# One of 47 FFN groups back from seven products to eight, its weight differences four slots later, and five filling matmuls instead of thirteen

## The chip, the cores and the metric

The kernel runs on one core of a Trainium2 chip. The metric is the device time of one execution in microseconds (us), of which the median over several runs is taken. One further execution is recorded by the hardware profiler; its rows give the durations used below. The core's engines are named as in the profile: PE (TensorE's matmuls), PEld (its weight loads), DVE (VectorE), ACT (ScalarE), POOL (GpSimd) and SP (SyncE, here only a queue that issues DMAs).

## The reference

```python
def _attn_ref(x, filt_r, filt_i):            # x: 8 x 3008 x 256
    X = np.fft.rfft(x, axis=1)
    F = (filt_r + 1j * filt_i)[None, :, :]
    return np.fft.irfft(X * F, n=x.shape[1], axis=1).astype(np.float32)

def _moe_ref(x, w_in, w_out):                # w_in 256 x 2048, w_out 2048 x 256
    h = np.maximum(x @ w_in, 0.0)
    return (h * h @ w_out).astype(np.float32)

# out = _moe_ref(_attn_ref(x, filt_r, filt_i).reshape(24064, 256), moe_w_in, moe_w_out)
```

A filter is applied to each of the 8 sequences in the frequency domain, along the 3008 tokens; then all 24064 tokens go through a feed-forward network (FFN) with a squared ReLU between its two matrices.

## The kernel before, in words

The Fourier transforms are done as matmuls with constant tables, in units: `unit_a` and `unit_b` go forward, `unit_b` multiplies on DVE with the filter (tile `prod`, L421) and POOL adds the two halves of a product by DMA, `unit_p` begins the way back and writes it to HBM (`dZ`), and `unit_y` ends it: it takes a tile `zt`, read back from `dZ` by `read_z` on SP's queue, and gives 376 of the 3008 tokens of `yt`, the FFN's input, in half of the 256 features (L497 on PE, L504 on ACT or L506 on DVE).

The FFN goes over 47 groups of 512 tokens, in slots, eight to a group. In slot 8g + k, `ffn_g1(g, k)` computes 256 of the 2048 hidden values of group g with four matmuls of 512 columns ("G1" below, L527, into `psH`), and ACT takes their ReLU into `h2` (L531, named `h` in the profile). In every second slot `ffn_sq` squares four tiles of `h2` on DVE (L538).

The second matrix comes a group later and in one of two forms. Groups in `SEVEN` take a seven-product form (Winograd's variant of Strassen's): token halves and hidden-tile parities make four quadrants, and so do the tile parity and column halves of W_out. `sums(g, k)` builds four sums and differences of quadrants of `h2` on DVE (L613 to L622, 128 x 2048 each), `products(g, k, s)` does 7 x 16 matmuls of 128 columns one slot later than the plain form would (L642), and the outputs `top` and `bot` are put together by four copies on ACT and three adds on DVE (L649 to L663). The differences of W_out (`sT`) that these products need are made once by `make_t`, four DVE subtractions of 128 x 1024 (L594). The other groups, before the change only the last, take the plain form: `ffn_g2` does eight matmuls of 256 columns per slot, 64 in all (L547), half of the hidden tiles in each slot, and `ffn_out` copies the result on ACT (L558) and stores it.

The order on every engine is the order of the program. The loop over the slots (L810) calls, in this order: `ffn_g1`, the Fourier units planned for the first half of the slot, `make_t` in its four slots, `products` or `ffn_g2`, the units planned for the second half, `ffn_out`, `sums`, `ffn_sq`, and the stores due. The plan (`fft_plan`) gives each unit its half slot by hand-written due times. For the first sequence, `unit_y` for n = 4 to 15 lies in slots 4 to 23, and n = 8 in slot 10; the second sequence's `unit_b` begins in slots 13, 14, 15 and 16.

Before the loop stands a prologue that transforms the first sequence. At its end, `read_z(0, 0)` and `read_z(0, 1)` are issued on SP; POOL waits for the first half of the first of them (`tiny`, L793) and then issues the two halves of the load of W_out (L321), which converts to 16 bits on the way. PE does `unit_a` for the second sequence, then 13 matmuls of zero weights with 512 columns into a bank that nobody reads (`fill`, L800), then `unit_y(0, 0)` to `unit_y(0, 3)`, and the loop begins.

PSUM tiles in the tag `psF` have two buffers, shared by `unit_b`, `unit_p` and `unit_y`; `psO` has two as well, for the outputs of both forms of the second matrix.

Of the kernel before, what the change touches and what calls it, by code (L numbers as in the profile page):

```python
# [110 lines left out]
def kernel(  # L111
# [16 lines left out]
    NG = T // TG  # L128
# [28 lines left out]
    def psF(name):  # L157
        return pps.tile([128, 512], F32, tag="psF", name=name, bufs=2)
# [352 lines left out]
    def ffn_g1(g, s):  # L511
        if s == 0:
            h2s[g] = p_h2.tile([128, NJT, TG], F16, tag="h2", name=f"h2_{g}")
        h2 = h2s[g]
        ps = psH(f"psH_{g}_{s}")
        segs = []
        t = g * TG
        while t < (g + 1) * TG:
            b, r = divmod(t, S)
            n = min((g + 1) * TG - t, S - r)  # L520
            segs.append((t - g * TG, b, r, n))
            t += n
        for i in range(2):
            jt = 2 * s + i
            for o, b, r, n in segs:
                for dt in range(2):
                    nc.tensor.matmul(ps[:, i, o:o + n],  # L527
                                     sWin[:, dt, jt * 128:(jt + 1) * 128],
                                     yts[b][:, dt, r:r + n],
                                     start=(dt == 0), stop=(dt == 1))  # L530
        nc.scalar.activation(out=h2[:, 2 * s:2 * s + 2, :], in_=ps, func=AF.Relu)  # L531

    def ffn_sq(g, s):
        n = 1 if g == NG - 1 else 2
        if (s + 1) % n:
            return
        v = h2s[g][:, 2 * (s + 1 - n):2 * s + 2, :]
        nc.vector.tensor_mul(out=v, in0=v, in1=v)  # L538

    def ffn_g2(g, s):  # L540
        t, half = divmod(s, 2)
        if s % 4 == 0:
            pso[g] = psO(f"psO_{g}_{s}")
        elif g == NG - 1 and half == 0:
            pso[g] = psF(f"psO_{g}_{s}").rearrange("p (a d) -> p a d", d=256)
        for jt in range(8 * half, 8 * half + 8):
            nc.tensor.matmul(pso[g][:, t % 2, :], h2s[g][:, jt, t * 128:(t + 1) * 128],  # L547
                             sWout[:, jt, :], start=(jt == 0), stop=(jt == NJT - 1))

    def ffn_out(g, s):  # L550

        step = 1 if g == NG - 1 else 2
        if (s + 1) % (2 * step):
            return
        n = s // 2 + 1 - step
        ost = p_out.tile([128, 2, 256], F32, tag="ost", name=f"ost_{g}_{s}")
        h0 = n % 2
        nc.scalar.copy(out=ost[:, h0:h0 + step, :], in_=pso[g][:, h0:h0 + step, :])  # L558
        store(g, n, step, ost)

    def store(g, n, step, ost):

        h0 = n % 2
        t0 = g * TG + n * 128
        if step == 2 and t0 // CLS == (t0 + 255) // CLS:
            pieces = [(0, 128, slice(0, 2), t0)]
        else:
            pieces = []
            for h in range(h0, h0 + step):
                a = t0 + 128 * (h - h0)  # L570
                cut = min(-a % CLS, 128) or 128
                pieces += [(p0, p1, h, a + p0) for p0, p1 in ((0, cut), (cut, 128)) if p1 > p0]
        for p0, p1, h, t in pieces:
            b, t = divmod(t, S)
            r, q = divmod(t, CLS)
            v = out[b * S:b * S + S, :].rearrange("(q r) c -> r q c", r=8)[r]
            if p1 - p0 == 128 and h != 0 and h != 1:
                nc.sync.dma_start(out=v[q:q + 256, :].rearrange("(h p) c -> p h c", p=128), in_=ost)
            else:
                nc.sync.dma_start(out=v[q:q + p1 - p0, :], in_=ost[p0:p1, h, :])  # L580
# [4 lines left out]
    def make_t(k):  # L585

        w = sWout.rearrange("p (q e) c -> p q e c", e=2)
        b11, b12 = w[:, :, 0, 0:128], w[:, :, 0, 128:256]
        b21, b22 = w[:, :, 1, 0:128], w[:, :, 1, 128:256]
        if k == 0:  # L590
            sg["t"] = p_t.tile([128, 4, 8, 128], F16, tag="t", name="sT")
        t = sg["t"]
        i0, i1 = ((b12, b11), (b22, t[:, 0]), (b22, b12), (b21, t[:, 1]))[k]
        nc.vector.tensor_sub(out=t[:, k], in0=i0, in1=i1)  # L594
        sg["w"] = {1: b11, 2: b21, 3: b22, 4: t[:, 3], 5: t[:, 0], 6: t[:, 1], 7: t[:, 2]}
# [5 lines left out]
    def sums(g, k):  # L601

        if k not in (0, 1, 2, 4):
            return
        a11, a12, a21, a22 = quads(g)
        if k == 0:
            sg[g] = {1: a11, 2: a12, 4: a22}
        f = sg[g]
        if k in (0, 2):
            f["s"] = p_x32.tile([128, 2, 8, D], F16, tag="x32", name=f"sum_{g}_{k}")  # L610
        t = f["s"][:, 0 if k in (0, 2) else 1]
        if k == 0:
            nc.vector.tensor_add(out=t, in0=a21, in1=a22)  # L613
            f[5] = t
        elif k == 1:
            nc.vector.tensor_sub(out=t, in0=f[5], in1=a11)  # L616
            f[6] = t
        elif k == 2:
            nc.vector.tensor_sub(out=t, in0=a11, in1=a21)  # L619
            f[7] = t  # L620
        else:
            nc.vector.tensor_sub(out=t, in0=a12, in1=f[6])  # L622
            f[3] = t
# [7 lines left out]
    def products(g, k, s):  # L631

        f = sg[g]
        for p, m0, m1 in PARTS[k]:
            if p == 1 and m0 == 0:
                f["x"] = psO(f"psX_{g}").rearrange("p a (t c) -> p a t c", t=2)
            if p == 2 and m0 == 0:
                f["y"] = psO(f"psY_{g}").rearrange("p a (t c) -> p a t c", t=2)
            o = f["x"][:, 0] if p in (1, 6, 7, 4) else f["y"][:, 0 if p == 2 else 1]
            for m in range(m0, m1):  # L640
                q, t = divmod(m, 2)
                nc.tensor.matmul(o[:, t, :], f[p][:, q, 128 * t:128 * t + 128], sg["w"][p][:, q, :],  # L642
                                 start=(m == 0 and p in (1, 2)), stop=(q == 7),
                                 skip_group_check=True)
            if m1 < 16:
                continue
            if p == 1:
                f["top"] = p_out.tile([128, 2, 256], F32, tag="ost", name=f"top_{g}")
                nc.scalar.copy(out=f["top"][:, :, 0:128], in_=o)  # L649
            elif p == 6:  # L650
                nc.scalar.copy(out=f["top"][:, :, 128:256], in_=o)
            elif p == 7:
                f["bot"] = p_out.tile([128, 2, 256], F32, tag="ost", name=f"bot_{g}")
                nc.scalar.copy(out=f["bot"][:, :, 128:256], in_=o)
            elif p == 2:
                for v, i in ((f["top"][:, :, 0:128], 0), (f["bot"][:, :, 128:256], 1)):
                    nc.vector.tensor_add(out=v, in0=f["y"][:, i], in1=v)  # L657
            elif p == 4:
                nc.scalar.copy(out=f["bot"][:, :, 0:128], in_=o)
                stores.append((s + 1, g, 2, f["bot"]))  # L660
            elif p == 3:
                v = f["top"][:, :, 128:256]
                nc.vector.tensor_add(out=v, in0=o, in1=v)  # L663
                stores.append((s + 1, g, 0, f["top"]))
# [64 lines left out]
    def run(plan, s, place):  # L729
        for f, *a in plan.get(2 * s + place, ()):  # L730
            f(*a)
# [64 lines left out]
    for c in range(4):  # L796
        unit_a(1, c)
    ps = psF("fill")
    for _ in range(13):
        nc.tensor.matmul(ps, zero, sSB[:, 0:4, :].rearrange("p a b -> p (a b)"),  # L800
                         start=True, stop=True)
    for n in range(4):
# [1 line left out]
    prologue[0] = False  # L804
    read_z(0, 2)

    SEVEN = range(NG - 1)
    work = fft_plan()

    for s in range((NG + 1) * SLOTS):  # L810
        g, k = divmod(s, SLOTS)
        if g < NG:
            ffn_g1(g, k)
        run(work, s, 0)
        if 8 <= s < 12:
            make_t(s - 8)
        if (s - 1) // SLOTS - 1 in SEVEN:
            products((s - 1) // SLOTS - 1, (s - 1) % SLOTS, s)
        if g > 0 and g - 1 not in SEVEN:
            ffn_g2(g - 1, k)  # L820
        run(work, s, 1)
        if g > 0 and g - 1 not in SEVEN:
            ffn_out(g - 1, k)
        if g - 1 in SEVEN:
            sums(g - 1, k)
        if g < NG:
            ffn_sq(g, k)
        while stores and stores[0][0] <= s:
            _, i, n, ost = stores.pop(0)
            store(i, n, 2, ost)  # L830
# [30 lines left out]
```

## Time and profile before

| | before |
|---|---|
| median of 4 runs | 758.73 us (758.31 to 759.98) |
| the profiled execution's own time | 759.1 us |
| its span, first to last instruction | 757.3 us |
| mean granted TensorE clock | 0.998 |
| busy: PE / DVE / ACT / POOL | 737.8 / 657.1 / 564.8 / 191.6 us |
| fills run from, to | 44.4 to 49.0 us |
| slot 0 begins (first G1 matmul) | 50.45 us |
| products of group 0 begin / of group 1 | 61.63 / 79.23 us |
| last group's plain products | 746.40 to 753.6 us |

Times within the profile count from the span's start. A busy share says how long an engine had an instruction under way; matmuls are pipelined, so that a busy PE need not be at its peak. "Idle before" in a row is the time that the engine waited ahead of it, and behind the arrow stands the instruction or transfer whose end released it. PEclk is the clock that TensorE was granted as a share of its full rate. The DMA share is the mean busy share of the core's 16 DMA engines; where many transfers overlap it can exceed 1.

### The profile page before, as it was taken

The page shows a single profiled execution, that of the slowest core. Times are in us where ns is not written, and L with a number is a line of the kernel's source. Part 1 is how long each engine was busy: PE and PEld are TensorE (multiplying, and loading weights), DVE is VectorE, ACT ScalarE, POOL GpSimd, SP SyncE. Part 2 cuts the span into 40 slices and gives each one's busy share as a digit, 9 for nine tenths or more (in the row PEclk, how much of TensorE's full clock was granted, in tenths as well). Part 3 has the DMA queues.
Part 4 walks back from the last instruction along what each step waited for, and adds up shares of the span by engine and source line. Part 5 has one row for each costly group of instructions (what it writes and reads, how often), then busy time and mean ns, then how long its engine had stood idle before and what let it go on. Part 6 is the DMA issues. An engine that isn't in the chain of part 4 may idle for free.

```text
span 757.3 us, 20205 instructions
## 1 busy us (share of the span) xinstructions
PE 737.8 (97%) x8511; PEld 536.3 (71%) x8511; DVE 657.1 (87%) x731; ACT 564.8 (75%) x808; POOL 191.6 (25%) x265
## 2 busy tenths in 40 slices
PE   7888999999999999999999999999999999999997
PEld 5535766777777777877678777787777777777776
DVE  5959998899899898989979998999988989888783
ACT  4867788778878777787777778777786777777773
POOL 2811750244222321232304224033311222000000
PEclk9999999999999999999999999999999999999999
DMA  9995898566785557746586546764447333321011
GB/s 351 306 192 172 143 184 234 163 118 120 165 221 120 96 128 176 181 103 136 105 219 128 125 100 135 230 130 101 103 113 200 81 77 92 98 86 42 30 57 57
DMA packets 103491, 106.36 MB, mean 140 GB/s; under 512 B 10352, under 2 KB 93552, under 8 KB 102248
## 3 DMA queue, kind: packets, MB, share of 16 engines
q1 hardware_dynamic: 83960, 81.83, 35.6%
q0 software_dynamic: 19296, 23.05, 21.5%
q8 instruction: 67, 1.10, 0.6%
q10 hardware_dynamic: 144, 0.18, 0.1%
q14 instruction: 24, 0.20, 0.1%
HBM read 57.80 MB, written 48.23 MB: 140 GB/s over the span
## 4 chain that ended last, share of the span: by engine, by line
PE 89%; DVE 5%; DMA 2%; ACT 2%; issue 1%; SPq 0%; DVEq 0%
PE psH L527 40%; PE psX L642 20%; PE psY L642 16%; PE psB L412 3%; PE psY L497 2%; PE psP L461 2%; PE psA L347 2%; DVE prod L421 1%; DMA zt<-dZ 1%; DMA xw<-in_x_dram 1%; DVE h L538 1%; PE psO L547 1%; ACT h L531 1%; PE psf L286 1%; PE fill L800 1%
## 5 line engine op out<-in xcount | busy, mean ns | idle before, releaser
L531 ACT ACTIVATE h<-psH 128x1024 f16<-128x1024 f32 x376 | 385.4, 1026 | 160.8 <-PE psH L527 159.8
L527 PE MATMUL psH<-yt,sWin 128*128 128x512 f16 (+7 forms) x1728 | 386.8, 351 | 1.2 <-ACT h L531 0.4
L538 DVE TENSOR_TENSOR h<-h 128x2048 f16<-128x2048 f16 (+1 forms) x192 | 230.1, 1199 | 45.6 <-ACT h L531 45.3
L429 POOL DMA_DIRECT2D prod<-prod x168 | 138.8, 968 | 429.3 <-DVE prod L421 426.9
L527 PEld LDWEIGHTS <-sWin 128*128 128x128 f16 x1728 | 149.1, 98 | 90.5 <-issue 3.0
L642 PEld LDWEIGHTS <-sum 128*128 128x128 f16 x2944 | 181.3, 98 | 26.2 <-issue 6.3
L642 PEld LDWEIGHTS <-h 128*128 128x128 f16 x2208 | 135.6, 98 | 24.5 <-issue 5.4
L421 DVE TENSOR_TENSOR prod<-psB,sF 128x1024 f16<-128x1024 f32 x84 | 102.4, 1220 | 11.9 <-PE psB L412 11.8
L642 PE MATMUL psX<-sT,sum 128*128 128x128 f16 x1472 | 104.7, 219 | 0.0
L642 PE MATMUL psY<-sT,sum 128*128 128x128 f16 x736 | 71.2, 219 | 0.0
L642 PE MATMUL psY<-sWout,sum 128*128 128x128 f16 x736 | 56.0, 219 | 1.4 <-DVE bot L657 1.4
L616 DVE TENSOR_TENSOR sum<-sum,h 128x2048 f16<-128x2048 f16 x46 | 56.2, 1221 | 0.8
L642 PE MATMUL psY<-sWout,h 128*128 128x128 f16 x736 | 56.2, 219 | 0.0
L642 PE MATMUL psX<-sT,h 128*128 128x128 f16 x736 | 56.1, 219 | 0.0
L622 DVE TENSOR_TENSOR sum<-h,sum 128x2048 f16<-128x2048 f16 x46 | 56.1, 1219 | 0.0
L619 DVE TENSOR_TENSOR sum<-h 128x2048 f16<-128x2048 f16 x46 | 56.0, 1218 | 0.0
L195 POOL DMA_DIRECT2D x<-in_x_dram x64 | 55.9, 1046 | 0.5 <-PE psA L347 0.5
L613 DVE TENSOR_TENSOR sum<-h 128x2048 f16<-128x2048 f16 x46 | 55.9, 1216 | 0.0
L463 ACT CAST ze<-psP 128x512 f16<-128x512 f32 x84 | 49.2, 586 | 1.3 <-PE psP L461 1.1
L642 PE MATMUL psX<-sWout,h 128*128 128x128 f16 x736 | 48.7, 219 | 0.0
L506 DVE CAST yt<-psY 128x376 f16<-128x376 f32 x62 | 33.7, 544 | 14.7 <-PE psY L497 14.5
L497 PE MATMUL psY<-sC,zt 112*128 112x94 f16 x512 | 42.3, 204 | 1.1 <-DMA zt<-dZ 0.7
(77 smaller groups left out, 547.2 us busy)
## 6 DMA issues: line engine op xcount, KB each, us to landing
zt<-dZ SPq DMA_DIRECT2D x64, 192.0 KB
dU<-u SPq DMA_DIRECT2D x56, 192.0 KB
prod<-prod POOLq DMA_DIRECT2D x168, 64.0 KB, 2.8
dZ<-ze SPq DMA_DIRECT2D x28, 384.0 KB
x<-in_x_dram POOLq DMA_DIRECT2D x48, 192.0 KB, 5.1
ut<-dU SPq DMA_DIRECT2D x7, 1024.0 KB
out_dram<-bot SPq DMA_DIRECT2D x32, 128.0 KB
out_dram<-top SPq DMA_DIRECT2D x16, 256.0 KB
```

What stands on the lines that cost most here:

```text
L195: nc.gpsimd.dma_start(out=t[64 * h + p0:64 * h + p1], in_=v[p0:p1, 8 * c:8 * c + 8, :])
L421: nc.vector.tensor_mul(out=prod[:, :, a:a + n, :], in0=ps.rearrange("p (a d) -> p a d", d=D)[:, a:a + n, :].unsqueeze(1) .to_broadcast([12 ...
L429: nc.gpsimd.dma_start(out=prod[64 * i:64 * i + 64, 0], in_=prod[64 - 64 * i:128 - 64 * i, 1], accum_op=mybir.AluOpType.add)
L497: nc.tensor.matmul(ps[:, 94 * jj:94 * jj + 94], zt[:, 4 * (g % 2) + jj, dt * 128:(dt + 1) * 128], sSY, start=True, stop=True)
L527: nc.tensor.matmul(ps[:, i, o:o + n], sWin[:, dt, jt * 128:(jt + 1) * 128], yts[b][:, dt, r:r + n], start=(dt == 0), stop=(dt == 1))
L531: nc.scalar.activation(out=h2[:, 2 * s:2 * s + 2, :], in_=ps, func=AF.Relu)
L538: nc.vector.tensor_mul(out=v, in0=v, in1=v)
L613: nc.vector.tensor_add(out=t, in0=a21, in1=a22)
L616: nc.vector.tensor_sub(out=t, in0=f[5], in1=a11)
L619: nc.vector.tensor_sub(out=t, in0=a11, in1=a21)
L622: nc.vector.tensor_sub(out=t, in0=a12, in1=f[6])
L642: nc.tensor.matmul(o[:, t, :], f[p][:, q, 128 * t:128 * t + 128], sg["w"][p][:, q, :], start=(m == 0 and p in (1, 2)), stop=(q == 7), skip ...
```

## The change

Group 0 leaves `SEVEN`, so that its part of the second matrix is done by `ffn_g2` and `ffn_out` in slots 8 to 15, and not by `sums` and `products` in slots 8 to 16. `make_t` moves from slots 8 to 11 to slots 12 to 15. The prologue issues 5 fills and not 13.

```diff
@@ -796,7 +796,7 @@
     for c in range(4):
         unit_a(1, c)
     ps = psF("fill")
-    for _ in range(13):
+    for _ in range(5):
         nc.tensor.matmul(ps, zero, sSB[:, 0:4, :].rearrange("p a b -> p (a b)"),
                          start=True, stop=True)
     for n in range(4):
@@ -804,7 +804,7 @@
     prologue[0] = False
     read_z(0, 2)
 
-    SEVEN = range(NG - 1)
+    SEVEN = range(1, NG - 1)
     work = fft_plan()
 
     for s in range((NG + 1) * SLOTS):
@@ -812,8 +812,8 @@
         if g < NG:
             ffn_g1(g, k)
         run(work, s, 0)
-        if 8 <= s < 12:
-            make_t(s - 8)
+        if 12 <= s < 16:
+            make_t(s - 12)
         if (s - 1) // SLOTS - 1 in SEVEN:
             products((s - 1) // SLOTS - 1, (s - 1) % SLOTS, s)
         if g > 0 and g - 1 not in SEVEN:
```

## The prediction

> **What bounds the kernel now.** I read the page's busy shares first, then the stretches around the edited lines (busy time by window), then the chain of waits through them, then the rows of the tiles touched.
>
> ```profile
> PE 737.8 (97%) x8511; PEld 536.3 (71%) x8511; DVE 657.1 (87%) x731; ACT 564.8 (75%) x808; POOL 191.6 (25%) x265
> ```
>
> ```profile
> core 0: us, PE busy (x) PEld busy (x) DVE busy (x) ACT busy (x) POOL busy (x), PEclk, DMA share, GB/s
> 41.00:44.40 3.40, 2.19 (x24) 0.60 (x20) 3.08 (x4) 3.40 (x9) 0.00 (x0) 1.00 0.50 155
> 44.40:47.80 3.40, 3.40 (x13) 1.20 (x10) 1.87 (x2) 0.79 (x2) 2.01 (x3) 0.50 0.94 199
> 47.80:50.45 2.65, 2.37 (x30) 1.68 (x29) 0.79 (x2) 0.94 (x2) 0.00 (x0) 1.00 1.05 197
> 50.45:59.60 9.15, 8.51 (x49) 3.95 (x49) 4.61 (x6) 7.55 (x10) 0.00 (x0) 1.00 1.27 235
> 59.60:78.20 18.60, 16.46 (x174) 11.43 (x174) 18.18 (x22) 12.07 (x17) 4.28 (x6) 1.00 0.49 146
> 78.20:94.00 15.80, 15.32 (x166) 11.07 (x164) 15.70 (x16) 11.99 (x20) 10.79 (x16) 1.00 0.87 146
> ...
> 139.00:740.00 601.00, 599.71 (x6916) 442.02 (x6914) 538.37 (x596) 458.32 (x652) 141.94 (x188) 1.00 0.52 123
> ```
>
> Over the whole span PE is the bound, but not where the edit lies. From 44.40 to 47.80 PE only runs fills, at a granted clock of 0.50. From 50.45 to 59.60 (slots 0 to 7) PE and ACT take turns. From 59.60 to 78.20 (slots 8 to 16) DVE is busy 18.18 of 18.60 us and PE 16.46; up to 94, DVE 15.70 of 15.80. After 139 PE has no idle time to speak of, so a lead that reaches that point stays to the end. The chain of waits says the same:
>
> ```profile
> 44.47 4.58 PE fill L800 x13
> ...
> 50.45 1.19 PE psH L527 x4
> ...
> 60.48 0.71 DVE h L538
> 61.19 0.43 issue
> 61.63 0.69 DVE sT L594
> 62.31 1.13 DVE sum L613
> ...
> 71.39 1.15 DVE prod L421
> ...
> 79.74 1.14 DVE sum L613
> ```
>
> The fills lie on the chain, and from 60.48 to 79.74 it is nearly all DVE. The rows for the costs:
>
> ```profile
> L800 PE MATMUL fill<-sSB,zero x13: 379/608/634, 44.4 to 48.7; 128*128 128x512 f16 x13
> L547 PE MATMUL psO<-sWout,h x64: 269/272/273, 746.4 to 753.3; 128*128 128x256 f16 x64
> L321 POOL DMA_DIRECT2D sWout<-in_moe_w_out_dram x2: 896/920/945, 45.7 to 46.6; - x2
> DMA to landing us min/median/max: 10.6/12.6/14.5
> ```
>
> **Part 1: eight fills fewer.** A fill lasts 608 ns at the half clock and 379 ns after 47.8; their weight loads start every 0.43 us until 47.79. Five fills end at 44.40 + 5 x 0.43 = 46.5. What they cover is the read of zt: the trace's DMA landings put the last packet of its second half at 46.93. So PE idles about 0.4 us, and unit_y(0, 0) starts at about 46.98 instead of 48.99. From there to the first G1 matmul (50.45) the trace has 1.46 us; the part before 47.8 (0.8 us) would run at half speed and take 0.4 us more. G1 then starts at 46.98 + 1.46 + 0.4 = 48.85, 1.6 us earlier. Slots 0 to 7 are an ACT/PE chain that moves as a block: slot 8 starts at 57.98 instead of 59.58.
>
> Whether the clock comes back at 47.8 is the unsure term. The stretch before it with PE busy 2.19 of 3.40 us was followed by half speed; 37.6 to 41.0, busy 2.64, was not. With the edit, 44.4 to 47.8 would be busy for about 3.0, so I take recovery at 47.8, and keep "a further 3.4 us at half speed" as the other end (up to 1.7 us).
>
> The Trainium skill (TensorE: Matmul & The Clock Gate, "What's actually happening") speaks against this edit: half clock is the default, restored after a busy window of about 3.4 us, and the windows run freely. The one half-speed stretch here, 3.4 us long, agrees. By that rule another run, with its windows lying elsewhere, could drop the clock at 46 to 47, when only five fills fill the window, and lose up to 1.7 us of the 1.6 us gained; no run here shows it.
>
> **Part 2: group 0 in the plain form.** Removed from PE: 112 products of 128 columns. Sixteen of them take 0.89 us in the chain of waits, 56 ns each: 6.2 us. Added: 64 matmuls of 256 columns; the last group's 64 take 7.16 us there, 112 ns each. PE does 0.9 us more. Removed from DVE: four sums at 1.13 us start to start (1.22 long) and three adds at 0.34, 5.5 us in all, on the engine that bounds slots 8 to 16. Removed from ACT: four copies of 0.37 to 0.39 us; added: two copies of double width. Bounds for one, from ze (128x512, 0.59 us) and the last group's ost (128x256, 0.37 us): 0.37 to 0.75; I take 0.59, the same width. ACT is busy 12.07 of 18.60 us there and hides it; without that cover it would cost 0.3 us a copy. The stores of group 0 leave SP at about 66 and 74 instead of 76 to 79. On SP nothing due is behind them until the dZ write at 87.
>
> The added wait is PE's on W_out. Slot 8 needs its first half (landed at 45.7 + 10.6 = 56.3); slot 9 needs the second, landed at 46.6 + 14.5 = 61.1 (61.16 by its last packet). Behind this wait on PE lie slot 10's G1 and all later products, so ACT and DVE wait with it. Neither landing depends on the fills: POOL issues them after the first half of zt. In numbers: slot 8: G1 takes 1.20 us (59.58 to 60.78 in the trace, the yt wait in it), 57.98 to 59.18; eight matmuls of 0.112 to 60.08. Slot 9: G1 0.86 to 60.94, wait to 61.21, eight matmuls to 62.11. So 0.27 us of the lead is lost to W_out. Slot 10: G1 to 62.97, and unit_y(0, 8) needs the third zt read, whose last packet landed at 62.98: no loss, but no cover either. Then 0.17 + 0.90 to 64.1. Slots 11 and 12: 1.93 us each, to 67.96. Slot 13: G1 0.86 and psB 0.22: the first product with sF can start at 69.1, instead of 71.30, since no backlog of sums stands before it. A lead of 2.2 us.
>
> **Part 3: make_t in slots 12 to 15.** Four subtractions of 0.69 us (0.61 start to start). Before, they sat among the sums in slots 8 to 11. Now one is done in DVE's idle time in slot 12, but three lie in slots 13 to 15 among the products with sF. From the first of these to the first sum of group 1 DVE has 8.35 us of back-to-back work now (71.30 to 79.65). Take away the three adds and a short wait (1.1), add three make_t (1.8): 9.05. Group 1's first sum starts at 69.1 + 9.05 = 78.15 instead of 79.65: a lead of 1.5 us. PE's lead there is larger: the last square of group 1 ends near 77.15, so products of group 1 start at 77.2 against 79.23, 2.0 us. DVE stays saturated up to 109, so its 1.5 counts; three short waits of DVE on PE at 93.0, 94.3 and 97.2 (0.14 + 0.21 + 0.18 = 0.5) can come back in part, as PE is ahead by 0.5 more: 1.5 to 2.0, and I take 1.7. Slot 16 now has no products; DVE is the later engine there, so that costs nothing.
>
> **Sum.** The profiled execution took 759.1 us (span 757.3, 1.8 around it): 759.1 - 1.7 = 757.4. The median of the runs is 0.4 lower, so I say 757.0, a gain of 0.23%. A difference under 0.2% (1.5 us) can't be told from none here.
>
> **Rivals.**
> A, the sum above: 757.0, its own range 755.6 to 757.9.
> B, PE alone counts: DVE, freed of 5.5 us, holds up nobody until 109. At slot 10 PE's lead is 0.4 us (G1 at 62.53 now, 62.11 then), and the 0.9 us of added matmul time is paid by then: 48 x 0.112 is left, as much as the 96 x 0.056 now. To it come PE's waits, 1.1 us before psB (71.2 to 72.6), 1.0 before the last product (74.9), and 0.5 up to 94: a gain of 3.0 us, 755.7. Against it: the DVE count of slots 13 to 16 above.
> C, the lead is pinned by transfers: W_out and the third zt read land in a stretch with a DMA share of 1.27, and later the reads for the second sequence (zt landing at 122.04, used at 123.01) leave 1.0 us. If these land no earlier, 0.4 to 1.0 us is left: 758.1. For it: both margins are near zero; against it: the later chain starts from products that move earlier with DVE.
> D, slower: five fills don't bring the clock back. Unit_y then takes 0.7 us longer (G1 from 49.5), and PE does a slot's G1 in 4 x 0.43 = 1.71 us instead of the 1.14 that slots 0 to 7 take each now: 0.57 us lost a slot. The wait on W_out takes back 0.27. With half speed up to 58.0, the end of a third further stretch of 3.4 us, that is 0.7 + 5 x 0.57 - 0.27 = 3.3 against a gain of 1.7, so 1.6 us slower: 760.3. Up to 61.4 it is seven slots, 2.7 us slower, 761.4. It decides from about 54 on (2.2 slots eat up the gain). Against it: at half speed G1 keeps PE fully busy, which ended the only half-speed stretch in the trace.
>
> **How the numbers follow.** A 0.45, B 0.14, C 0.24, D 0.17 (and whatever else delays PE in slots 0 to 16). Faster by over 0.2% (below 757.2): all of B and nine tenths of A, 0.56 with a little of C. Within: most of C and the rest of A, 0.27. Slower: D, 0.17. The range reaches from B's far end, 755.3, to 760.3, which leaves out the worse half of D.
>
> **What would show it.** Right: five fills ending near 46.5, unit_y at 47.0, the clock at 1.00 from 47.8; the first G1 near 48.9; psO of group 0 starting in slot 8 near 59.2 with a short wait before its second eight, near 61.2; DVE idle between 62 and 69; the first sum of group 1 near 78.2; the same distance to the end as before. Wrong: half speed after 47.8 (D), products with sF starting before 68 or PE without waits from 62 to 94 (B), PE waiting on zt near 63 or 121 (C).

## The result, and the profile after

| | before | changed |
|---|---|---|
| median | 759.21 us (56 runs) | 757.02 us (37 runs) |
| profiled execution / its span | 759.1 / 757.3 us | 757.0 / 755.2 us |

The ratio is 0.9972, 95% interval 0.9965 to 0.9979: 2.1 us less (1.6 to 2.7), with a median of 757.0 forecast. Run once more later, beside other kernels, the changed kernel gave 0.9981 (0.9968 to 0.9993), 1.4 us less.

The stretches of the changed kernel, cut as in the prediction (width, then busy time of PE, PEld, DVE, ACT and POOL, PEclk, DMA share, GB/s):

```profile
41.00:44.40 3.40, 2.19 (x28) 0.70 (x20) 2.85 (x4) 3.40 (x9) 0.00 (x0) 1.00 0.52 166
44.40:47.80 3.40, 3.13 (x18) 1.44 (x18) 2.10 (x2) 1.05 (x4) 2.01 (x3) 0.57 0.86 190
47.80:50.45 2.65, 2.37 (x24) 1.52 (x22) 1.10 (x2) 1.00 (x3) 0.00 (x0) 0.91 1.06 204
59.60:78.20 18.60, 18.32 (x150) 12.64 (x148) 13.44 (x16) 12.98 (x17) 5.62 (x7) 1.00 0.61 172
78.20:94.00 15.80, 14.52 (x156) 10.45 (x154) 15.49 (x16) 11.23 (x17) 10.95 (x15) 1.00 0.85 138
```

From 59.6 to 78.2 the bound has changed hands: PE is busy 18.32 of 18.60 us (16.46 before), DVE 13.44 (18.18 before). From 78.2 to 94 DVE is nearly as full as it was (15.49 us, 15.70 before), and PE has more idle time, not less. The clock was at half speed twice: from 24.37 to 27.79, ahead of everything that the edit touches and not so in the kernel before, and from 44.85 to 48.27. The chain of waits shows where the hand-over lies:

```profile
43.93 3.20 DMA zt<-dZ
47.13 0.14 issue
47.27 0.47 PE psY L497 x4
...
49.16 1.18 PE psH L527 x4
...
59.65 0.87 PE psO L547 x8
60.52 0.86 PE psH L527 x4
61.38 0.87 PE psO L547 x8
...
68.84 0.23 PE psB L412 x2
69.07 0.02 issue
69.10 1.23 DVE prod L421
```

The chain now starts with the zt read instead of the fills, runs over PE through slots 8 to 13, and goes over to DVE at 69.1. DVE's rows from there:

```profile
67.70 0.69 DVE L594 TENSOR_TENSOR sT<-sWout 128x1024 f16<-128x1024 f16 x1
69.10 1.23 DVE L421 TENSOR_TENSOR prod<-psB,sF 128x1024 f16<-128x1024 f32 x1 [0.71 <-PE psB L412]
70.24 0.68 DVE L594 TENSOR_TENSOR sT<-sWout,sT 128x1024 f16<-128x1024 f16 x1
...
73.56 0.68 DVE L594 TENSOR_TENSOR sT<-sWout 128x1024 f16<-128x1024 f16 x1
...
75.29 0.68 DVE L594 TENSOR_TENSOR sT<-sWout,sT 128x1024 f16<-128x1024 f16 x1
...
78.16 1.22 DVE L613 TENSOR_TENSOR sum<-h 128x2048 f16<-128x2048 f16 x1
```

One make_t falls into idle time ahead of 69.1; three stand in the row between the first product with sF (69.10) and the first sum of group 1 (78.16). In the kernel before, the same two rows were:

```profile
71.30 1.22 DVE L421 TENSOR_TENSOR prod<-psB,sF 128x1024 f16<-128x1024 f32 x1
...
79.65 1.22 DVE L613 TENSOR_TENSOR sum<-h 128x2048 f16<-128x2048 f16 x1
```

To follow the gain through the kernel, take the starts of the ReLU rows (L531), one per slot, of both profiles:

| slot | 0 | 9 | 13 | 15 | 17 | 20 | 20 to 276 | from 282 |
|---|---|---|---|---|---|---|---|---|
| lead of the changed kernel, us | 1.29 | 0.47 | 0.16 | 1.57 | 2.86 | 1.49 | 1.44 to 1.49 | 2.00 |

PE gives back 0.8 us in slot 8 and 0.3 more up to slot 13, since it does more matmul time earlier; then the leads of 2 to 3 us come from the products that DVE no longer holds up; and by slot 20 DVE has taken back what exceeds its own lead: 1.49 us. The last 0.5 us appears at 578 us, where PE waited 0.7 us for a zt read before and 0.2 after. This is the row of before:

```profile
578.40 0.33 PE L497 MATMUL psY<-sC,zt 112*128 112x94 f16 x4 [0.71 <-DMA zt<-dZ]
```

Against before, four of the kernels below lose 0.3 to 1.0 us at this read. Yet PE waits for it in all four profiles with group 0 in the seven-product form (0.47 to 1.70 us) and not at all in seven of the ten with the plain form (0.19, 1.41 and 1.72 us in the others). Whether this 0.5 us is chance or a part of the change stays open.

### The profile page after: what moved, and what is told of

Same layout as the page of the kernel before. It is cut to its first block, busy times and chain, and to the rows that moved or that the text cites. A ratio compares the mean times of both kernels' runs of the same rounds, so it can differ in the third digit from the quotient of the medians.

```text
span 755.2 us, 20081 instructions
## 1 busy us (share of the span) xinstructions
PE 738.0 (98%) x8455; PEld 535.8 (71%) x8455; DVE 650.9 (86%) x724; ACT 564.6 (75%) x806; POOL 191.2 (25%) x265
## 3 DMA queue, kind: packets, MB, share of 16 engines
q8 instruction: 66, 1.08, 0.6%
HBM read 57.80 MB, written 48.23 MB: 140 GB/s over the span
## 4 chain that ended last, share of the span: by engine, by line
PE 89%; DVE 5%; DMA 3%; ACT 2%; issue 1%; SPq 1%; DVEq 0%; ACTq 0%
PE psH L527 40%; PE psX L642 20%; PE psY L642 16%; PE psB L412 3%; PE psY L497 3%; PE psP L461 2%; PE psA L347 2%; PE psO L547 2%; DMA zt<-dZ 1%; DVE prod L421 1%; DVE h L538 1%; DMA xw<-in_x_dram 1%; ACT h L531 1%; PE psf L286 1%; PE psP L445 1%
## 5 line engine op out<-in xcount | busy, mean ns | idle before, releaser
L531 ACT ACTIVATE h<-psH 128x1024 f16<-128x1024 f32 x376 | 385.5, 1026 | 160.5 <-PE psH L527 159.0
L642 PEld LDWEIGHTS <-sum 128*128 128x128 f16 x2880 | 177.4, 98 | 24.8 <-issue 5.3
L642 PEld LDWEIGHTS <-h 128*128 128x128 f16 x2160 | 132.6, 98 | 24.3 <-issue 5.3
L642 PE MATMUL psX<-sT,sum 128*128 128x128 f16 x1440 | 102.4, 219 | 0.0
L619 DVE TENSOR_TENSOR sum<-h 128x2048 f16<-128x2048 f16 x45 | 54.8, 1218 | 0.0
L613 DVE TENSOR_TENSOR sum<-h 128x2048 f16<-128x2048 f16 x45 | 54.7, 1216 | 0.0
L642 PE MATMUL psX<-sWout,h 128*128 128x128 f16 x720 | 47.8, 219 | 0.0
```

## The experiments

Profiles differ in when the prologue gets to its end, so times are counted from the landing of the second half of the first zt read. "First sum" is group 1's first sum on DVE, "product" the first product with sF. All in us.

| kernel | ratio to before (95%) | zt lands | to first ReLU | to product | product to first sum | zt to ReLU of slot 30 |
|---|---|---|---|---|---|---|
| before | 1 | 46.93 | 4.73 | 24.37 | 8.35 | 60.48 |
| changed | 0.9972 (0.9965 to 0.9979) | 47.13 | 3.24 | 21.97 | 9.06 | 58.79 |
| changed, again | 0.9981 (0.9968 to 0.9993) | 47.16 | 3.25 | 22.80 | 9.06 | 59.62 |
| 5 fills alone | 1.0006 (0.9991 to 1.0020) | 45.79 | 3.02 | 23.04 | 8.35 | 59.14 |
| 5 fills alone, again | 1.0010 (0.9994 to 1.0027) | 45.52 | 3.04 | 23.74 | 8.36 | 59.85 |
| changed, 13 fills | 0.9984 (0.9971 to 0.9997) | 46.85 | 4.81 | 23.54 | 9.06 | 60.37 |
| changed, no fill | 0.9975 (0.9963 to 0.9986) | 46.90 | 4.30 | 23.46 | 9.06 | 60.28 |
| changed, make_t early | 0.9958 (0.9941 to 0.9974) | 46.86 | 3.36 | 22.42 | 7.62 | 57.80 |
| the same, again | 0.9954 (0.9935 to 0.9972) | 48.42 | 2.79 | 22.55 | 7.63 | 57.95 |
| changed, make_t early on POOL | 0.9965 (0.9951 to 0.9980) | 47.84 | 2.79 | 22.36 | 8.11 | 58.24 |
| changed, make_t doubled | 0.9997 (0.9980 to 1.0015) | 46.88 | 2.79 | 21.52 | 11.25 | 60.52 |
| before, clock kept up | 0.9974 (0.9960 to 0.9987) | 46.03 | 2.91 | 23.52 | 8.35 | 59.63 |
| changed, clock kept up | 0.9969 (0.9955 to 0.9984) | 48.48 | 2.79 | 22.42 | 9.06 | 59.25 |
| make_t early, clock kept up | 0.9967 (0.9953 to 0.9982) | 46.91 | 3.03 | 21.97 | 7.62 | 57.50 |

**Is DVE the bound after slot 13?** First, make_t back in slots 8 to 11:

```diff
-        if 12 <= s < 16:
-            make_t(s - 12)
+        if 8 <= s < 12:
+            make_t(s - 8)
```

> The changed kernel with make_t in slots 8 to 11 as before. Theory: DVE is idle for 2.1 us ahead of 62.5 and 2.4 us ahead of 66.1, so make_t fits there once W_out has landed (60.4 to 61.2) and costs nothing; between the first product with sF (69.1) and the first sum of group 1 DVE has 7.2 us of work and not 9.05, so the first sum stands at about 76.4 and not 78.16; the lead against before in the steady part is 2.3 to 3.0 us and not 1.5, as PE's 1.2 us wait at 81.7 goes or shrinks: 0.8 to 1.5 us under the changed kernel. Rival (PE alone counts): no difference to the changed kernel. Rival (make_t waits for W_out in front of a square): the square at 62.5 comes later, and with it nothing else.

DVE's rows of this kernel:

```profile
61.27 0.69 DVE L594 TENSOR_TENSOR sT<-sWout 128x1024 f16<-128x1024 f16 x1 [0.99 <-DMA sWout<-in_moe_w_out_dram]
61.99 0.69 DVE L594 TENSOR_TENSOR sT<-sWout,sT 128x1024 f16<-128x1024 f16 x1
62.60 1.22 DVE L538 TENSOR_TENSOR h<-h 128x2048 f16<-128x2048 f16 x1
...
69.28 1.22 DVE L421 TENSOR_TENSOR prod<-psB,sF 128x1024 f16<-128x1024 f32 x1 [1.31 <-PE psB L412]
...
76.90 1.22 DVE L613 TENSOR_TENSOR sum<-h 128x2048 f16<-128x2048 f16 x1
```

The first make_t waits for W_out in time that DVE has to spare, all four are done by 65.0, and the first sum comes 7.62 us after the product, not 9.06; three make_t of 0.60 us start to start, less 0.35 us of new waits on PE. From zt to slot 30 it is 1.0 us less than in the changed kernel. Both kernels once more, on one chip:

> The changed kernel with make_t in slots 8 to 11, once more on the same chip as the changed kernel. Theory: 0.8 to 1.5 us under the changed kernel, 2.5 to 4 us under before. Rival (DVE does not bound): equal to the changed kernel.

> The changed kernel once more, to stand beside the one with make_t early on the same chip, and for a second profile. Theory: 1.6 to 2.7 us under before; in the profile the first product with sF 21.9 to 22.6 us after the second half of zt has landed, as far as the clock is at half speed at the same place or not at all. Rival (the gain of the first profile was luck): the same time as before.

The medians were 755.53 us with make_t early, 757.82 for the changed kernel and 759.75 before. Make_t early beats both, here by 2.3 us under the changed kernel (six runs of 754.7 to 757.4 against twelve of 755.9 to 759.3). That is more than the 0.8 to 1.5 expected and than the 1.0 of the first two profiles. The next kernel doubles the suspect:

```diff
-        nc.vector.tensor_sub(out=t[:, k], in0=i0, in1=i1)
+        for _ in range(2):
+            nc.vector.tensor_sub(out=t[:, k], in0=i0, in1=i1)
```

> The changed kernel with each of the four subtractions of make_t done twice (slots 12 to 15). Theory (DVE bounds slots 13 to 31 of the changed kernel): four more at 0.6 us, three or four of them between the first product with sF and the first sum of group 1: that sum comes 1.8 to 2.4 us later measured from the first product with sF (9.06 us in the changed kernel, 10.9 to 11.5 then), and the kernel is 1.5 to 2.4 us slower than the changed one. Rival (PE alone counts, DVE has slack): under 0.5 us.

```profile
68.40 1.23 DVE L421 TENSOR_TENSOR prod<-psB,sF 128x1024 f16<-128x1024 f32 x1
...
79.65 1.22 DVE L614 TENSOR_TENSOR sum<-h 128x2048 f16<-128x2048 f16 x1
```

From product to first sum it took 11.25 us, 2.19 more, as expected; the median (759.18) is 1.4 us above the changed kernel's, a little under the 1.5 expected, and the gain against before is gone. Taking DVE work out of this row and adding to it both move the time: rival B (PE alone) falls. A fourth kernel moves make_t to POOL, in slots 8 to 11:

```diff
-        nc.vector.tensor_sub(out=t[:, k], in0=i0, in1=i1)
+        nc.gpsimd.tensor_sub(out=t[:, k], in0=i0, in1=i1)
```

> The changed kernel with make_t in slots 8 to 11 and on POOL, which has nothing to do from 47.6 to 70.6. Theory: as with make_t early on DVE, 0.8 to 1.5 us under the changed kernel, and no better than that by more than 0.2 us, since DVE had room in slots 8 to 11. Rival (a shared port: POOL's work slows DVE): squares and products longer than 1.22 us beside it, and less gain. Rival (POOL takes over 3 us for one): the products of group 1 that need the differences (slot 18) wait, and it is slower than the changed kernel.

Its rows for the subtractions, by line (minimum, median and maximum in ns, then first and last start):

```profile
L594 POOL TENSOR_TENSOR sT<-sWout x2: 2117/2120/2123, 61.9 to 67.1; 128x1024 f16<-128x1024 f16 x2
L594 POOL TENSOR_TENSOR sT<-sWout,sT x2: 2987/3050/3112, 64.1 to 69.2; 128x1024 f16<-128x1024 f16 x2
```

POOL takes 2.1 us for two of them and 3.0 and 3.1 us for the other two, against 0.69 on DVE, and is done at 72.27. It is no better than make_t early on DVE, as expected, and by the slot 30 column 0.3 to 0.4 us worse; its ratio lies 0.5 us under that of the changed kernel, short of the 0.8 expected. The expectation's rival, POOL's work slowing DVE, did occur, in the squares:

```profile
62.74 2.39 DVE L538 TENSOR_TENSOR h<-h 128x2048 f16<-128x2048 f16 x1 [2.05 <-ACT h L531]
...
67.64 2.65 DVE L538 TENSOR_TENSOR h<-h 128x2048 f16<-128x2048 f16 x1
70.21 1.21 DVE L421 TENSOR_TENSOR prod<-psB,sF 128x1024 f16<-128x1024 f32 x1
...
71.80 1.55 DVE L538 TENSOR_TENSOR h<-h 128x2048 f16<-128x2048 f16 x1
```

They take 2.39, 2.65 and 1.55 us instead of 1.22. Each of them began while POOL was subtracting and ended 1.08 us after that subtraction (at 65.13, 70.28 and 73.35; the subtractions ended at 64.05, 69.20 and 72.27). Each of the two long subtractions ended 1.99 us after a square (at 67.12 and 72.27). So squares and subtractions took turns, while the product at 70.21 kept its 1.21 us. The first two long squares did not delay the first product with sF (22.36 us after zt; 22.42 and 22.55 with make_t early on DVE). The third stands in the row from it to the first sum, which took 8.11 us and not 7.62.

**What are the fills worth?** The fill cut alone, twice:

> The kernel before with 5 fills, nothing else changed. Theory (DVE bounds slots 8 to 31, fed by the W_out load): unit_y and slot 0 come 1.3 to 1.6 us earlier, but the first make_t then waits for W_out, which lands at 60.4 to 61.2, so the DVE chain (first make_t at 61.63 before) moves by only 0.4 to 1.1 us and that is the gain: 0.4 to 1.1 us. Rival (PE alone counts): the whole 1.3 to 1.6 us. Rival (half clock stays): no gain or slower.

> The kernel before with 5 fills, once more: its profile showed a lead of 1.3 us after the zt read, its timed runs none. Theory now: fewer fills leave PE idle from 46.5 on, so more runs meet a second stretch at half clock; with DVE waiting for W_out and then bounding slots 9 to 31, what is won in one run is lost in another: within 0.7 us of before, with a granted clock of 0.995 or less in half of the runs or more. Rival (the fill cut is worth its 0.4 to 1.1 us): that much under before.

Both profiles show the lead of the first theory or a little more (1.3 and 0.6 us at slot 30, counted from zt), and in both DVE waits for W_out; this is the row of the second:

```profile
59.57 0.69 DVE L594 TENSOR_TENSOR sT<-sWout 128x1024 f16<-128x1024 f16 x1 [0.96 <-DMA sWout<-in_moe_w_out_dram]
```

The timed runs show nothing: both ratios are above 1, with 1 inside their intervals, which leave room for a gain of 0.7 us at most. The two profiled executions were the fastest of their twelve, so that the lead in them is not that of the median. The gain expected first was not found. Of the second expectation the time held (medians 0.6 us above before); the clock did not quite, as 5 of the 12 runs have a mean granted clock of 0.995 or less and half or more was expected. Of both kernels' 24 runs it is 13, against 30 of 93 runs of before. That fewer fills are the reason is not shown: the changed kernel with 13 fills has 7 such runs of 12. And in ten of the fourteen profiles, in all ten with group 0 in the plain form and in no other, the clock is at half speed for one or two periods between 23.2 and 30.7 us, ahead of every fill. Why these ten have it stays open, and so does why the fill cut alone shows no gain.

> The changed kernel with 13 fills again. Theory: PE is the bound from slot 8 to slot 13, so a slot 0 that is 1.3 us later (50.45) puts the first product with sF at about 70.4 and the first sum of group 1 at 79.4 to 79.5, against 78.16 with 5 fills and 79.65 before: gain against before 0.1 to 0.4 us, so that the two parts are worth more together than alone. Rival (PE alone counts, DVE relieved): PE's waits of 2.1 us between 59.6 and 78.2 go in any case, gain 1 us or more. Rival (parts add): 1.5 us less the gain of the fills alone.

In the profile this came out as expected (product at 70.39, first sum at 79.45, a lead of 0.2 at slot 30), but the timed runs gained 1.2 us (0.2 to 2.2), more than the 0.1 to 0.4 expected and nearer to its two rivals, a gain of 1 us or more and a sum of the two parts; the interval excludes none of them. A profile is one run with one place of the half-speed stretch; that in other runs the 13 fills go at full speed and end earlier is likely, but was not shown here. The plain form alone is therefore most of the gain that the timed runs show; whether the fill cut adds to it lies inside the intervals of the two (0.9971 to 0.9997 and 0.9965 to 0.9979).

> The changed kernel with no fill at all. Theory (the fills feed the clock gate, and PE bounds slots 8 to 13, so that a late slot 0 costs its full size): PE idles from 44.4 to 47, half speed lasts past 47.8 or starts in the middle of unit_y and slot 0; unit_y and the first G1 take 1 to 1.7 us more, and the kernel is 0.8 to 1.7 us slower than the changed one. Rival (the fills only hide a wait): the same time as the changed kernel, since zt's landing (47) and not the fills starts unit_y in both.

Two stretches of the kernel without fills:

```profile
44.40:45.80 1.40, 0.40 (x6) 0.11 (x2) 1.40 (x2) 0.90 (x2) 0.18 (x1) 1.00 0.68 205
45.80:52.60 6.80, 5.51 (x30) 3.06 (x31) 1.69 (x3) 1.97 (x3) 1.83 (x2) 0.50 1.11 193
```

Half speed lasts from 45.8 to 52.6, two periods, and slot 30 comes 1.5 us later than in the changed kernel, as the theory says. The median of the timed runs shows no such loss (0.9975), against the 0.8 to 1.7 us expected; the profiled execution was the slowest of its twelve. With 13, 5 and no fills the ratios of the changed kernel are 0.9984, 0.9972 and 0.9975: the timed runs show no effect of the number of fills.

**Keeping the clock up.** Six more fills where PE waits in `unit_a`, and 12 at the end:

```diff
     for c in range(4):
         unit_a(1, c)
+        if c < 3:
+            ps = psF(f"mid{c}") if c % 2 else psO(f"mid{c}").rearrange("p a d -> p (a d)")
+            for _ in range(2):
+                nc.tensor.matmul(ps, zero, sSB[:, 0:4, :].rearrange("p a b -> p (a b)"),
+                                 start=True, stop=True)
     ps = psF("fill")
-    for _ in range(13):
+    for _ in range(12):
```

> The kernel before with six fills more, two after each of the first three units of unit_a, where PE waits on ACT and DVE, and 12 fills instead of 13 at the end. Theory: PE's activity does not drop between 41 and 44.4, no half-clock stretch follows, 12 fills at 0.216 end near 47.0 and slot 0 starts 1.5 to 2 us earlier than in the profile of before; but DVE's first make_t waits for W_out (60.4 to 61.2), so that against before only 0.2 to 0.8 us are gained. Rival (PE alone counts): 1.5 us or more. Rival (the clock drops in any case): half speed again, no gain.

The stretches around the fills in this kernel:

```profile
41.00:44.40 3.40, 3.40 (x28) 1.22 (x25) 3.40 (x4) 3.21 (x7) 0.00 (x0) 1.00 0.62 174
44.40:47.80 3.40, 3.12 (x34) 2.03 (x33) 1.72 (x3) 1.11 (x3) 2.01 (x3) 1.00 1.02 231
```

With PE busy all through 41.0 to 44.4 the clock stays at 1.00 where it fell to 0.50 before. The first ReLU comes 1.8 us earlier, of which 0.85 is left at product and slot 30, for DVE's first make_t waited 0.88 us for W_out. The timed gain is 2.0 us (1.0 to 3.0), more than the 0.2 to 0.8 expected. By the timed runs this kernel, with group 0 still in the seven-product form, gains as much as the change does (0.9974 and 0.9972).

> The changed kernel with the same six fills more and 12 fills instead of 5 at the end. Theory: no half-clock stretch between 40 and 50, first ReLU 2.7 to 2.9 us after the second half of zt has landed (3.24 in the changed kernel, 4.73 before); this lead passes through the PE-bound slots 8 to 13: 0.3 to 0.6 us under the changed kernel, unless the wait on W_out in slot 9 takes it (then 0.0 to 0.2). Rival (a longer row of fills delays slot 0 as before): the time of the changed kernel with 13 fills.

> The changed kernel with make_t in slots 8 to 11 and the same fills as the kernel with the clock kept up (six more in unit_a, 12 at the end). Theory: the two gains add, as DVE is no longer the bound from slot 13 on: 0.3 to 0.6 us under the kernel with make_t early alone, about 755.2, the fastest of all. Rival (W_out's landing pins slot 9): no better than make_t early alone.

The changed kernel is not measurably faster with its clock kept up (0.9969), and make_t early not either (0.9967 against 0.9958 and 0.9954), though the latter's profile has the shortest way to slot 30 of all. The expected 0.3 to 0.6 us was not found; with intervals of 1.1 us to either side it can't be excluded. The runs of the changed kernel with its clock kept up do differ with the granted clock: four with 0.999 or 1.0 took 755.5 to 755.8 us, three with 0.995 took 758.5 to 759.8. The profiled one is among these three: its clock was at half speed from 23.25 to 30.08, ahead of all fills, and its zt landed at 48.48. Over all profiles, zt landed at 47.84 to 48.48 us where the clock was at half speed for two periods there, at 46.85 to 47.16 with one, and at 45.52 to 46.93 with none. Times counted from zt leave this cost out.

## Why the prediction was right

**The DVE count held to 0.1 us.** Forecast: first product with sF at 69.1, 9.05 us of DVE work from it to the first sum, that sum at 78.15, a lead of 1.5. Measured: 69.10, 9.06, 78.16, 1.49. The doubled and the early make_t show that this term moves the time.

**Three terms ahead of it were off and cancelled, by luck.** Forecast were a start of slot 0 1.6 us earlier, and 0.27 us of it lost to W_out. The lead was 1.29, for two small reasons: zt landed at 47.13, not 46.93, and the clock came back at 48.27, not 47.8. W_out landed at 60.43 instead of 61.16 and PE needed it at 61.22: no wait. 1.6 - 0.27 = 1.33 against 1.29 - 0. The ACT copies took 592 ns, with 0.59 forecast.

**The allowance of 0.2 us was wrong.** The idle time of DVE that was to come back did not: its waits of 0.21 and 0.18 us are still there (at 93.0 and 95.9 now). PE's lead at the first products of group 1 was larger than forecast, 2.86 and not 2.0, as they began at 76.38, before the last square was done at 77.11, which the forecast had taken for their condition. But PE lost it in a wait of 1.0 us, up to 82.97, for the product with sF that DVE began at 81.69. So the profile's own account is 1.5 from the change and 0.5 from the read at 578.

**That the median is 757.0 to the digit is luck.** The forecast took 1.7 us from a base of 758.73; the base of the comparison is 759.21, and 2.1 us went. The two timed comparisons, 2.1 and 1.4 us, hold 1.5 only in the second interval and just miss it in the first (1.6 to 2.7); what the rest is stays open. Nor do the timed runs confirm the first part of the forecast, the 1.6 us of the fills: the fill cut alone shows no gain, and the change without it 1.2 of the 2.1 us. The path, PE to slot 13 and DVE from there, is what the profiles and the runs with make_t early and doubled show.

**The rivals.** B fell with make_t early and doubled; its waits had been read a little high, too (0.98, 0.81 and 0.41 us in the trace, which with its 0.4 us of lead makes 2.6 and not 3.0). C did not occur here: the third zt read landed at 62.75 and was used at 62.96, so its margin was 0.2. That was close: in the second profile of make_t early PE waits 0.9 us for W_out, and in the changed kernel with its clock kept up 0.6 us for zt. D did not occur in the first profile, but its mechanism is real. The second profile of the changed kernel has its half-speed stretch in slot 0 and after it, when PE had been busy for only 2.15 of the 3.40 us from 44.4 (1.89 of the last 3.41 us, from 45.90). Its stretches:

```profile
44.40:47.80 3.40, 2.15 (x22) 1.19 (x22) 2.15 (x2) 1.20 (x4) 2.00 (x3) 1.00 0.88 199
47.80:49.30 1.50, 1.22 (x17) 0.76 (x15) 1.10 (x2) 0.81 (x2) 0.01 (x1) 1.00 1.01 231
49.30:52.70 3.40, 3.40 (x9) 1.21 (x8) 0.00 (x0) 1.60 (x2) 0.00 (x0) 0.50 1.29 184
```

PE runs nine matmuls in 3.40 us at 0.50, and the product came 22.80 us after zt, 0.83 later than in the first profile, whose stretch began at 44.85. That is what the Trainium skill (TensorE: Matmul & The Clock Gate, "What's actually happening") made one expect of other runs: windows of 3413 ns that run freely. In all profiles here the clock changes of one run lie multiples of 3.41 us apart, at a place that differs from run to run. Of the eight profiles with five fills this is the only one in which half speed begins after the fills. By these two profiles the stretch in this place cost 0.8 us more than the one at 44.85, and it ended after one period, in which PE was full.

## What to carry to other kernels

Find the engine that bounds the stage, not the kernel: here 5.5 us were taken off DVE and 1.5 arrived, because PE bounds the five slots before and DVE, with three moved subtractions in its row, those after. Count the row of back-to-back instructions between two events that depend on each other: it came out at 9.06 us with 9.05 forecast, while the lead it started from was right only because errors cancelled. Place small extra work into the idle time that the same change opens: make_t left in slots 8 to 11 is worth another 1.0 us by the first profiles. And time a change in many runs before its parts are priced from one profile: the fill cut has a lead of 0.6 to 1.3 us in its profiles and none in its runs.

## What the runs showed of the hardware that was not expected

The clock fell to half not only after idle time: PE was busy 2.19 of 3.40 us (64%) before it fell, with small matmuls of 47 rows and 64 columns in it. The busy time alone does not tell: in the same profile PE was busy 1.78 of 3.41 us from 20.50 to 23.91 and the clock stayed, and with make_t doubled it was busy 1.98 of 3.41 us from 45.17 to 48.58 and the clock stayed. For the return the profiles do agree: after 23.2 us, a half-speed period with PE busy for 2.94 of 3.41 us or less was followed by another, and one with 2.96 or more was not.

The same kernel's runs differ by 3 to 5 us, twice the effect studied here, in part with the number and place of such stretches, so one profile is no measure of what a fill is worth. The mean clock does not fix the time either: runs of the changed kernel with 0.995 took 756.5 to 760.3 us.

A subtraction that takes DVE 0.69 us took POOL 2.1 us, and 3.0 and 3.1 us where a square on DVE ran into it; three such squares took 1.55 to 2.65 us instead of 1.22.
